# Attention, MoE and MoE2 fused on one core: MoE2's second products by seven in all four groups of sets 0 and 1, recombined at the set's end

## The chip, the cores and the metric

The kernel runs on one core of one Trainium2 chip. The metric is device time in microseconds (us) of one execution, as the median of repeated runs. The core has five engines with a queue each, and each queue runs strictly in its own order: TensorE (PE, matrix products), VectorE (DVE), ScalarE (ACT), GpSimd (POOL) and SyncE (SP, which here issues nearly all transfers). They wait for each other by semaphores.

## What is computed

The reference, cut to what matters:

```python
# attention in chunks of 64 rows: B, H, S, D = 4, 8, 576, 64
scores = q_c @ k_c.T / sqrt(D);  attn = softmax(scores);  x = attn @ v_c   # -> x: 2304 x 512
# MoE, 4 experts, hidden size 1024
p = domain_probs / (domain_probs.sum(-1) + 1e-9)
out = sum_e p[:, e] * (relu(x @ w1[e]) @ w2[e])                            # 2304 x 512
# MoE2, hidden size 2048
h = out @ w_in;  g = h * clip(h + 3, 0, 6) / 6
result = g @ w_out                                                         # 2304 x 512
```

## The kernel before

**Precision.** PE multiplies in a rounded form of float32 (fp32r). Each operand is split into a high part (a cast on ACT) and a low part (the difference, on DVE or POOL), and each product is three matmuls: high by high, high by low, low by high. So every operand costs one ACT instruction and one DVE or POOL instruction before PE may use it.

**Sets, groups, units.** The 2304 tokens are three sets of 768, and each set is two halves of N = 384 tokens (index z). The hidden columns are groups of 512: eight for MoE (phase 0), four for MoE2 (phase 1). A unit is one group of one set: first the h products (x by the first weights), then a gate, then the y products (gate by the second weights). Phase 0 runs set 0, 1, 2, then phase 1 runs set 0, 1, 2. The attention of set 0 fills the start of the program, and that of sets 1 and 2 is done in small pieces beside MoE.

**Products by seven.** All h products but those of the first unit use a scheme of Strassen's kind: seven half-size products instead of eight, of sums of blocks. In `h_pair` (L971 and after) they are asked for in the order P1, P6, P7, P5, P2, P4, P3, twice for each unit (two pairs), six matmuls of 384 columns each (L989), and DVE recombines them (L999). Their x operands are built once for each set by `build_x`: seven high parts on ACT (L703, 768 columns, or L707), fourteen low halves on DVE (L711, 384 columns), and eight differences of 384 columns on DVE (L717), 22 DVE steps in all. P6 needs the difference called t2 (both halves, in place in the tile xs), and P5 and P4 need differences too. The seven operands have one buffer each (the slots of x7), so that an operand of the next set can be written only after the last product of the present set has read that slot.

**The y products.** In MoE2 the units g = 0, 1, 2 of every set do their y products by seven as well (`y_sevens`, L1167: 126 matmuls of 256 columns), with sums of gate blocks made by `gate_sums` (L1112) and split by `parts` (L1103, L1105). The seven results M1 to M7 are added up over the groups in tiles called totals (acc, tri, vr, qr, kr; copies at L1180, additions at L1182), and `recombine` (L1196, seven additions of 256 columns for each of three row blocks j) turns them into plain accumulators at the end of group 2. Group 3 is plain (`y_unit`, L1221: 72 matmuls of 512 columns): its results are added to the accumulators by `finish` (L1265) and sent out (L1282).

**The order.** Nothing is ordered by hand. `Plan` takes every operation with an engine, a length by a formula, a due time and its dependencies, plays them through, and emits the instructions in the order of the starts it found. On an engine the ready operation with the earliest due time goes first. Operations marked `pair` (both inputs in SBUF) are put 8 us later on DVE while POOL is busy (`YIELD`), and are taken to last longer by a share of what POOL still has to do (`SHARED`). The tables at the top of the file (L20 and after) shift due times and lengths. `build_x` for phase 1 is due 12 us ahead of its unit.

Of the kernel before, what the change touches and what calls it, by code (L numbers as in the profile page):

```python
# [18 lines left out]

W_LEAST = 2.0 ** -15  # L20
W_MOST = 122880.0 - 2.0 ** -6
Y0 = 18.74
SLACK = (6.73, 4.93, 5.97, 0.92)
LOADS = (((0.0, 0.0), (0.4, 0.55)), ((4.0, 4.0), (4.1, 4.1)), ((9.0, 9.0), (9.1, 9.1)))

ITEMS = (56.47, 23.57, -37.2, 3.52)
STAGES = (12.74, -112.55)
LEAD = (14.98, 23.38, 6.6, 8.16)
LOAD = 13.67
BACK = (("pyy", "ppp"), ("pyp", "ppp"))  # L30
CO = ("POOL","POOL","DVE")
FIRST = 271.53
KEPT = 1.15
EARLY = 12.94
RGAP = 7.28
PLAIN_STAY = (1, 3)
STAY = (("A12", 0), ("A12", 1), ("A22", 0))
S4_STAY = (0,)
SUMS = 1.53
YB = ("yyy","ahy","yhh","ahh")  # L40
LATER = 3.06
LO = 0.81
VLOADS = (1.0, 6.0, 12.0)
SH = (0.0, 0.0, 0.0)
BANKS = (("hhhhh", "yahay"), ("ayaay", "yyyay"), ("ayaay", "ayaay"))
# [2 lines left out]
def raw(ap):  # L48
    return ap.bitcast(F32)
# [23 lines left out]
class Plan:  # L73
# [3 lines left out]
    LAT = 0.3  # L77
    EVERY = 0.6
    DENSE = 7.7
    CALM = 5.19  # L80
    LANES = 8
    SHARED = 0.87
    YIELD = 8

# [16 lines left out]
    def run(self):  # L101
        free = dict(self.caps)
        ready = {e: [] for e in ("PE", "DVE", "ACT", "POOL", "SP")}
        busy = dict.fromkeys(ready, 0.0)
# [16 lines left out]
        done, position, now = 0, 0, 0.0  # L121
# [32 lines left out]
        def choose(e):  # L154
            if e == "PE":
                nxt = self.main[position] if position < len(self.main) else None
                able = nxt is not None and nxt.left == 0 and any(r is nxt for r in ready[e]) and room(nxt)
                sides = sorted((r for r in ready[e] if r.side), key=lambda r: (r.due, r.n))
                for s in sides:
                    if (s.due <= now or not able) and fits(s):  # L160
                        return s
                return nxt if able else None
            able = sorted(ready[e], key=lambda r: (r.due, r.n))
            if e == "DVE" and busy["POOL"] > now + 0.15 and able:

# [24 lines left out]
        while done < len(self.ops):  # L190
# [19 lines left out]
            for e in ready:  # L210
                if busy[e] > now + 1e-9 or not (ready[e] or e == "PE" and now < self.warm):
                    continue
                o = choose(e)
                if o is None:
                    if e == "PE" and filled < now < self.warm:
                        fill(now)
                        filled = now + (self.EVERY if now >= self.DENSE else 0.0)
                    continue
                ready[e].remove(o)
                for b in o.new:  # L220
                    free[b.tag] -= 1
                    heads[b.tag] += 1
                o.start = now
                busy[e] = now + o.us
                if o.pair and e == "DVE":

                    busy[e] += self.SHARED * max(busy["POOL"] - now, 0.0)
                if e == "PE" and not o.side:
                    position += 1
                end = busy[e]  # L230
                if o.lag:
                    pipe = max(pipe, end) + o.lag
                    end = pipe + 1.9 + o.slack
                    sent.append(pipe + 1.9)
                    seq += 1
                    heapq.heappush(events, (sent[-1], seq, 2, o))
                o.end = end
                seq += 1
                heapq.heappush(events, (end, seq, 1, o))
                seq += 1  # L240
                heapq.heappush(events, (busy[e], seq, 2, o))
# [16 lines left out]
def fused_kernel(ctx: ExitStack, tc: tile.TileContext, q, k, v, probs, w1, w2, win, wout, out):  # L258
# [5 lines left out]
    P = 128  # L264
# [93 lines left out]
    HP = 42  # L358

    YS = 14  # L360
    by_seven = lambda u: u[0] == 1 and u[2] < G2 - 1
    hus_of = lambda u: 48 * mm(2 * u[4]) if u[4] < N else 2 * HP * mm(N)
    START = 22.0
    clock, at = START, {}
# [458 lines left out]
    def split_y(ph, g, R, ld, due):  # L823
# [23 lines left out]
        T3 = sub(s3, r(1, 1), r(0, 1), ld, [R], 4.1)  # L847
        operand("M7", whole(s3), [s3], [T3], 5)
        operand("M3", r(1, 1), [R], ld, 6)
        return los  # L850

    def weights(ph, si, g):
# [5 lines left out]
        if (ph, si) != (0, 0):  # L858
# [2 lines left out]
                wready[key, name] = op("SP", 0.35, lambda b=b, name=name: nc.sync.dma_start(out=raw(b.t), in_=raw(kept[ph, g, name])), t - LEAD[0] + j, [stored[ph, g, name]], [b], lag=1.35, hold=hold)  # L861
            for n_, f in enumerate(YO if by_seven((*key, 0, N)) else FO):
                tag = YO.get(f, "wy")
                if tag != "e":
                    b = wo[key, "y", f] = buf(tag)
                    wready[key, "y", f] = op("SP", 0.35, lambda b=b, f=f: nc.sync.dma_start(out=raw(b.t), in_=raw(kept[ph, g, f])), t_y - LEAD[3] + n_, [stored[ph, g, f]], [b], lag=1.35, hold=hold_y)
# [280 lines left out]
    def y_sevens(u):  # L1147
# [6 lines left out]
        for q_, pair in enumerate(Y_PAIRS):  # L1154
# [19 lines left out]
            for j in range(NJ):  # L1174
# [6 lines left out]
                else:  # L1181
                    x = op("DVE", dve(w) + 0.08, lambda T=T, p=ps[j], w=w: nc.vector.tensor_tensor(out=T.t[:, :w], in0=p.t[:, :w], in1=T.t[:, :w], op=ALU.add), t + n_ * one + LATER - soon(u), [last[j], before], (), [T, ps[j]])  # L1182
                totals[k_] = (T, x)
        if g == G2 - 2:
            for j in range(NJ):
                recombine(si, j, t + n_ * one - soon(u) + RGAP * j, CO[j])

    def recombine(si, j, due, eng):

# [17 lines left out]
    def y_unit(u, z, ending=False):  # L1207
# [8 lines left out]
        for f, j in todo:  # L1216
            W, (G, lo, o) = wo[key, "y", f], gts[u, f, z]

            def fn(f=f, j=j, W=W, G=G, o=o):
                for i, (a, b) in enumerate(HL):  # L1220
# [1 line left out]
                        ps[j].t, G.t[:, a, o + j * P:o + (j + 1) * P], W.t[:, b, :],  # L1222
                        start=f == FO[0] and i == 0, stop=f == FO[-1] and i == len(HL) - 1,
                    )
            last[j] = op("PE", 3 * mm(512), fn, t, [wready[key, "y", f], lo], [ps[j]] if f == FO[0] else (), [W, G, ps[j]])
        end = t + len(js) * GF * 3 * mm(512)
        for j in js:
            finish(u, z, j + c0 // P, ps[j], last[j], end - (len(js) - 1 - j) * 3 * mm(512) * (GF if ending else 1), ending and j == len(js) - 1)
# [159 lines left out]
    for n_, u in enumerate(units):  # L1388
        ph, si, g, c0, n = u
        if ph == 1 and g == 0:  # L1390
# [3 lines left out]
            for b in range(P // R32):  # L1394
# [2 lines left out]
                    in_=x2s[si][:, b::P // R32].rearrange("r k z t -> r k (z t)"),  # L1397
                )
                lds.append(op("SP", 0.5, load, t - 30, x2ready[si], () if b else [X], [X], lag=1.0, hold=t - 60))
            build_x((1, si), lds, t - 12)  # L1400
        if is_plain(u):
            for f in range(GF):
                for zs in ((0, 1),) if n < N and n_ else ((0,), (1,)) if n_ else ():
# [51 lines left out]
```

## Time and profile before

| | before |
|---|---|
| median of 3 runs | 1178.86 us (1178.58 to 1183.39) |
| the profiled execution | 1178.26 us, span 1176.4 us |
| PE busy | 1160.3 us, 99% |
| DVE / ACT / POOL busy | 744.9 / 491.1 / 517.8 us |
| granted TensorE clock | 1.0 over the whole span (2.4 GHz) |
| DMA | 317.04 MB, mean 269 GB/s |

PE is the engine to look at: whatever adds or removes PE work, or makes PE wait, moves the end, and busy time on the others does so only through a wait of PE. The span minus PE's busy time is 16.1 us; most of that lies in the first 60 us and in the last 4. In MoE2, from 812.8 us on, PE has no gap at all before the tail.

### The profile page before, as it was taken

To read this page: it belongs to the slowest core of one execution; us is meant where nothing else is said; L and a number is where in the kernel's file an instruction comes from. 1 tells how busy PE (TensorE), PEld (TensorE's weight loads), DVE (VectorE), ACT (ScalarE), POOL (GpSimd) and SP (SyncE) were. 2 spreads that over 40 slices of the span, in tenths; PEclk is the share of its full clock that TensorE was granted. 3 is DMA by queue.
4 is the path that set the end of the run, shared out by engine and by line. 5 is a ranking of instruction groups with operands and counts; after the bars stand their busy time and mean duration, and the time that the engine had idled before them with its cause. 6 is when DMAs were issued, how large, how long until landed. Compare 5 with 4: busy or idle time off the path is not lost.

```text
span 1176.4 us, 20820 instructions
## 1 busy us (share of the span) xinstructions
PE 1160.3 (99%) x7488; PEld 1067.0 (91%) x7488; DVE 744.9 (63%) x1465; ACT 491.1 (42%) x1178; POOL 517.8 (44%) x458
## 2 busy tenths in 40 slices
PE   7999999999999999999999999999999999999998
PEld 7899988889998888888999999888999899989997
DVE  5565455458655666679645555468478846884685
ACT  5754444445344332435232333233534453345332
POOL 3576656555242253536243434341447044704470
PEclk9999999999999999999999999999999999999999
DMA  9678888768887998887978787987797678768751
GB/s 248 221 275 289 306 262 297 271 232 314 292 293 244 294 344 306 281 293 258 332 270 309 253 304 243 307 331 248 275 296 251 229 269 291 264 224 278 251 179 55
DMA packets 155783, 317.04 MB, mean 269 GB/s; under 512 B 70688, under 2 KB 77088, under 8 KB 155680
## 3 DMA queue, kind: packets, MB, share of 16 engines
q1 hardware_dynamic: 153936, 314.01, 78.8%
q10 hardware_dynamic: 1744, 1.70, 0.5%
q8 instruction: 59, 0.97, 0.3%
q14 instruction: 44, 0.36, 0.1%
HBM read 232.30 MB, written 83.36 MB: 268 GB/s over the span
## 4 chain that ended last, share of the span: by engine, by line
PE 92%; DVE 3%; DMA 2%; issue 1%; SPq 0%; ACT 0%; POOL 0%; DVEq 0%; POOLq 0%; ACTq 0%
PE h L989 40%; PE y L1221 36%; PE y L1167 5%; PE h L1167 4%; PE a L1167 2%; DMA k<-wp 2%; PE h L1048 2%; DVE x L711 1%; DMA wy<-k 1%; PE y L318 1%; PE a L567 1%; PE y L487 0%; PE h L576 0%; DVE gt L1073 0%; DVE xs L717 0%
## 5 line engine op out<-in xcount | busy, mean ns | idle before, releaser
L989 PE MATMUL h<-x,wh 128*128 128x384 f32 x2940 | 522.6, 335 | 2.4 <-DVE c L999 1.0
L989 PEld LDWEIGHTS h<-x,wh 128*128 128x128 f32 x2940 | 509.6, 188 | 7.7 <-DVE c L999 2.3
L1221 PE MATMUL y<-wy,gt 128*128 128x512 f32 x1944 | 454.2, 391 | 2.7 <-DVE acc L1258 2.6
L1221 PEld LDWEIGHTS y<-wy,gt 128*128 128x128 f32 x1944 | 362.2, 188 | 78.9 <-DVE acc L1258 4.0
L1258 DVE SCALAR_TENSOR_TENSOR acc<-y,pn,acc 128x512 f32<-128x512 f32 x126 | 89.0, 749 | 125.5 <-PE y L1221 125.3
L1105 POOL TENSOR_TENSOR gt<-t,gt 128x384 fp32r<-128x384 f32 x54 | 54.5, 1017 | 187.4 <-ACT gt L1103 187.1
L999 DVE TENSOR_TENSOR h<-h,c 128x384 f32<-128x384 f32 x152 | 84.5, 562 | 43.4 <-PE h L989 42.3
L1072 ACT ACTIVATE gt<-h 128x384 fp32r<-128x384 f32 (+1 forms) x150 | 68.8, 486 | 100.2 <-DVE h L999 99.5
L925 POOL TENSOR_TENSOR w<-w,rh 128x512 f32<-128x512 f32 x28 | 37.1, 1326 | 154.3 <-DVE rh L922 110.2
L999 DVE TENSOR_TENSOR c<-h,p 128x384 f32<-128x384 f32 x70 | 38.8, 554 | 91.9 <-PE h L989 62.3
L1073 DVE SCALAR_TENSOR_TENSOR gt<-h,gt 128x384 fp32r<-128x384 f32 (+1 forms) x150 | 76.6, 540 | 31.3 <-ACT gt L1072 29.6
L1006 ACT COPY p<-h 128x384 f32<-128x384 f32 x70 | 33.6, 480 | 124.3 <-PE h L989 123.9
L782 POOL TENSOR_TENSOR wp<-t,wp 128x512 fp32r<-128x512 f32 x36 | 47.1, 1308 | 72.4 <-ACT wp L780 72.4
L1080 ACT ACTIVATE t<-h,half 128x384 f32<-128x384 f32 x84 | 45.9, 579 | 53.8 <-DVE h L999 42.1
L782 POOL TENSOR_TENSOR wy<-t,wy 128x512 fp32r<-128x512 f32 x32 | 41.7, 1310 | 38.6 <-ACT wy L780 37.3
L782 POOL TENSOR_TENSOR wp<-rh,wp 128x512 fp32r<-128x512 f32 x24 | 32.1, 1336 | 55.8 <-ACT wp L780 55.8
L1167 PE MATMUL y<-wy,gt 128*128 128x256 f32 x432 | 56.1, 283 | 0.0
L1167 PEld LDWEIGHTS y<-wy,gt 128*128 128x128 f32 x432 | 54.1, 191 | 0.0
L780 ACT CAST wp<-t 128x512 fp32r<-128x512 f32 x36 | 22.4, 623 | 67.7 <-DMA k<-wp 47.3
L999 DVE TENSOR_TENSOR c<-h,c 128x384 f32<-128x384 f32 x70 | 38.8, 554 | 18.0 <-PE h L989 17.4
L711 DVE TENSOR_TENSOR x<-xs,x 128x384 fp32r<-128x384 f32 x66 | 42.8, 669 | 1.6 <-ACT x L703 1.6
L1103 ACT CAST gt<-t 128x384 fp32r<-128x384 f32 x66 | 32.7, 513 | 24.8 <-POOL t L1112 19.0
(209 smaller groups left out, 1435.7 us busy)
## 6 DMA issues: line engine op xcount, KB each, us to landing
wh<-k SPq DMA_DIRECT2D x196, 512.0 KB, 5.9
wy<-k SPq DMA_DIRECT2D x112, 512.0 KB, 5.2
k<-wp SPq DMA_DIRECT2D x60, 512.0 KB, 6.3
k<-wh SPq DMA_DIRECT2D x49, 512.0 KB, 3.6
k<-wy SPq DMA_DIRECT2D x32, 512.0 KB, 4.7
wp<-k SPq DMA_DIRECT2D x18, 512.0 KB, 4.4
t<-in_moe_w_dram SPq DMA_DIRECT2D x32, 256.0 KB, 4.4
rh<-in_moe_w_dram SPq DMA_DIRECT2D x8, 1024.0 KB, 7.7
```

The costliest lines, as they stand in the source:

```text
L711: lo = lambda k=k: nc.vector.tensor_tensor(out=b.t[:, 1, k], in0=src[k](), in1=raw(b.t[:, 0, k]), op=ALU.subtract)
L782: return op(eng, gps(512) if eng == "POOL" else dve(512), lambda: e.tensor_tensor(out=view(b.t[:, 1]), in0=read(), in1=raw(view(b.t[:, 0]) ...
L925: nc.gpsimd.tensor_tensor(out=low(), in0=low(), in1=dst(), op=ALU.mult)
L989: nc.tensor.matmul(acc.t[:, :n], W.t[:, a, k_ * 256 + pr_ * P:k_ * 256 + (pr_ + 1) * P], X.t[:, b, k_, cs], start=new and first, stop=last ...
L999: add = lambda out, x, y: (lambda: nc.vector.tensor_tensor(out=out(), in0=x(), in1=y(), op=ALU.add))
L1072: hi = op("ACT", act(n), lambda: nc.scalar.activation(hi_(), src(), AF.Relu), due, after, [G], bufs)
L1073: lo = op("DVE", dve(n), lambda: nc.vector.scalar_tensor_tensor(out=lo_(), in0=src(), scalar=0.0, in1=raw(hi_()), op0=ALU.max, op1=ALU.sub ...
L1080: x = op("ACT", act(n), lambda: nc.scalar.activation(r_(), src(), AF.Relu, bias=half, scale=1.0 / 6.0), due, after, [R], bufs)
L1105: lo = op(eng, dve(N) if eng == "DVE" else gps(N), lambda: e.tensor_tensor(out=where()[:, 1], in0=r_(), in1=raw(where()[:, 0]), op=ALU.sub ...
L1167: nc.tensor.matmul(ps[j].t[:, 256 * i:256 * i + 256], Gs[k][2]()[:, a, j * P:(j + 1) * P], part(b)[:, 256 * k:256 * k + 256], start=k == 0 ...
L1221: nc.tensor.matmul(ps[j].t, G.t[:, a, o + j * P:o + (j + 1) * P], W.t[:, b, :], start=f == FO[0] and i == 0, stop=f == FO[-1] and i == len ...
L1258: fn = lambda: nc.vector.scalar_tensor_tensor(out=A.t, in0=ps.t, scalar=p, in1=A.t, op0=ALU.mult, op1=ALU.add)
```

## The change

What it does, part by part:

- `by_seven` now holds for all groups of MoE2 but the last group of the last set. So group 3 of sets 0 and 1 does its y products by seven, and its weights are split into seven blocks (`split_y`) instead of four plain ones. For the plain group of set 2, `split_y` also stores M0, and `weights` puts each plain block together from two halves (two loads of 256 columns).
- `recombine` moves to the end of group 3 in sets 0 and 1, and the outputs are sent right after it from `y_sevens`. In set 2 it stays at the end of group 2. All three row blocks are recombined on POOL (`CO`); before, the third was on DVE.
- In `Plan`, `YIELD` and `SHARED` take effect only after 60 us of the plan (`BEGUN`), so that the first attention items are ordered by due times alone.
- `build_x` for phase 1 is due 22.88 us (`XD`) ahead instead of 12, and about twenty numbers of the tables differ.

The diff, cut to its core (lines of after.py are 3 to 19 higher than those of before.py: L711, L717, L999, L1182, L1196 become L714, L720, L1012, L1195, L1214):

```diff
-CO = ("POOL","POOL","DVE")
+CO = ("POOL","POOL","POOL")
+XD = 22.88
+RD = 4.75
...
+    BEGUN = 60
...
-            if e == "DVE" and busy["POOL"] > now + 0.15 and able:
+            if e == "DVE" and now > self.BEGUN and busy["POOL"] > now + 0.15 and able:
...
-                if o.pair and e == "DVE":
+                if o.pair and e == "DVE" and now > self.BEGUN:
...
-    by_seven = lambda u: u[0] == 1 and u[2] < G2 - 1
+    by_seven = lambda u: u[0] == 1 and u[1:3] != (NSET - 1, G2 - 1)
...
+        if not by_seven((ph, NSET - 1, g, 0, N)):
+            operand("M0", r(0, 1), [R], ld, 7)
...
+                if ph and f not in YO:
+                    b = wo[key, "y", f] = buf(tag)
+                    blocks = wready[key, "y", f] = []
+                    for d, name in enumerate((("M1", "M0"), ("M2", "M3"))[f % 2]):
+                        fn = lambda b=b, d=d, name=name, k=f // 2: nc.sync.dma_start(out=raw(b.t)[:, :, 256 * d:256 * d + 256], in_=raw(kept[ph, g, name])[:, :, 256 * k:256 * k + 256])
+                        blocks.append(op("SP", 0.35, fn, t_y - LEAD[3] + n_, [stored[ph, g, name], *blocks], () if d else [b], [b], lag=0.7, hold=hold_y))
+                    continue
...
-        if g == G2 - 2:
+        if g == G2 - 1 - (si == NSET - 1):
             for j in range(NJ):
-                recombine(si, j, t + n_ * one - soon(u) + RGAP * j, CO[j])
+                due = t + n_ * one - soon(u) + RGAP * j + RD
+                recombine(si, j, due, CO[j])
+                for z in range(2 if g == G2 - 1 else 0):
+                    A = accs[1, si, z, j]
+                    for ps_, rows in out_runs(si, z, j):
+                        op("SP", 0.5, lambda A=A, ps_=ps_, rows=rows: nc.sync.dma_start(out=rows, in_=A.t[ps_]), due + 24, [aready[1, si, z, j]], (), [A], lag=1.3 * (ps_.stop - ps_.start) / P)
...
-            build_x((1, si), lds, t - 12)
+            build_x((1, si), lds, t - XD)
```

**Where instructions move: DVE at the end of MoE2's set 0.** Before, these are the last steps for set 1's x operands (L717 differences, L711 low halves), the additions of group 3's results (L1265), and the first two sums of the next unit's h products (L999):

```order
L1265 TENSOR_TENSOR acc<-y,acc 128x512 x3
L717 TENSOR_TENSOR xs<-xs 128x384
L711 TENSOR_TENSOR x_65<-xs,x_65 128x384
L717 TENSOR_TENSOR xs<-xs 128x384
L711 TENSOR_TENSOR x_65<-xs,x_65 128x384 x2
L717 TENSOR_TENSOR xs<-xs 128x384
L711 TENSOR_TENSOR x_65<-xs,x_65 128x384 x5
L1265 TENSOR_TENSOR acc<-y,acc 128x512 x3
L999 TENSOR_TENSOR c<-h,p_10452 128x384
L999 TENSOR_TENSOR c<-h,c 128x384
```

Now, on the same engine and at the same place; the first row adds M3's last result of the unit (its PE product is the unit's last):

```order
L1195 TENSOR_TENSOR kr<-h,kr 128x256
L720 TENSOR_TENSOR xs<-xs 128x384
L714 TENSOR_TENSOR x_65<-xs,x_65 128x384
L720 TENSOR_TENSOR xs<-xs 128x384
L714 TENSOR_TENSOR x_65<-xs,x_65 128x384 x3
L720 TENSOR_TENSOR xs<-xs 128x384
L714 TENSOR_TENSOR x_65<-xs,x_65 128x384 x2
L720 TENSOR_TENSOR xs<-xs 128x384
L714 TENSOR_TENSOR x_65<-xs,x_65 128x384
L1012 TENSOR_TENSOR c<-h,p_10530 128x384
L1012 TENSOR_TENSOR c<-h,c 128x384
L714 TENSOR_TENSOR x_65<-xs,x_65 128x384 x2
```

Thirteen of the 22 x steps now stand behind the unit's last addition, and eleven of them ahead of the next unit's first sum. The end of set 1 has the same rows. On POOL, the 21 additions of `recombine` stand in one row there, between the last split of the unit and the first of the next.

**The same place on ACT.** Before, the casts for the x operands (L703), then the copy of the next unit's first product P1 (L1006):

```order
L1103 CAST gt<-h 128x384 x2
L1080 ACTIVATE t<-h,half 128x384 x2
L1103 CAST gt<-h 128x384 x2
L703 CAST x_65<-xs 128x768 x4
L1006 COPY p_10452<-h 128x384
L1080 ACTIVATE t<-h,half 128x384 x2
```

Now (L706 is the cast, L1019 the copy):

```order
L1116 CAST rh<-t 128x384
L1116 CAST w_10439<-h 128x384
L706 CAST x_65<-xs 128x768
L1019 COPY p_10530<-h 128x384
L706 CAST x_65<-xs 128x768 x3
L1093 ACTIVATE t<-h,half 128x384 x2
```

Three casts, those of P6, P5 and P4, now stand behind the copy of P1's result.

**DVE in the first attention items.** Before; L755 makes the low part of an x operand for the first unit, L529 to L559 belong to attention items:

```order
L557 TENSOR_REDUCE st<-e 128x8
L558 TENSOR_TENSOR st<-st,least 128x8
L559 RECIPROCAL st<-st 128x8
L529 TENSOR_REDUCE st<-y 128x4 x2
L755 TENSOR_TENSOR x_65<-xs,x_65 128x2x2x128
L533 TENSOR_TENSOR st<-st,minus 128x8
```

Now:

```order
L560 TENSOR_REDUCE st<-e 128x8
L561 TENSOR_TENSOR st<-st,least 128x8
L562 RECIPROCAL st<-st 128x8
L758 TENSOR_TENSOR x_65<-xs,x_65 128x2x2x128
L532 TENSOR_REDUCE st<-y 128x4 x2
L536 TENSOR_TENSOR st<-st,minus 128x8
```

The low part moved ahead of the two maxima. On POOL at the same place the weighing of an item (L563) moved ahead of the first split of a second weight (L782).

## Rows read from the trace of the kernel before

**Rows 1.** The page, part 1: busy us (share of the span) and instructions.

```profile
PE 1160.3 (99%) x7488; PEld 1067.0 (91%) x7488; DVE 744.9 (63%) x1465; ACT 491.1 (42%) x1178; POOL 517.8 (44%) x458
```

**Rows 2.** Waits of PE: who waited for whom, us in total, times, longest.

```profile
PE y L1221 <- DVE acc L1258: 2.6, 2, 1.4
PE h L1048 <- DVE x L755: 1.6, 1, 1.6
```

**Rows 3.** Windows: us, busy of each engine, clock, DMA share and GB/s.

```profile
20.00:40.00 20.00, 18.16 (x290) 15.59 (x288) 10.96 (x27) 14.49 (x46) 9.78 (x10) 1.00 1.00 287
528.00:561.00 33.00, 31.48 (x156) 27.64 (x155) 31.04 (x51) 16.47 (x32) 18.72 (x13) 1.00 0.78 269
700.00:804.00 104.00, 102.22 (x506) 90.80 (x504) 62.77 (x118) 31.85 (x61) 38.85 (x30) 1.00 0.88 307
812.80:932.80 120.00, 120.00 (x787) 116.97 (x787) 88.26 (x172) 54.31 (x109) 50.02 (x53) 1.00 0.77 258
```

**Rows 4.** Windows of a unit by seven and of set 0's plain unit.

```profile
842.47:872.12 29.65, 29.65 (x211) 29.65 (x211) 20.19 (x38) 11.91 (x25) 12.97 (x13) 1.00 0.73 261
901.76:932.79 31.03, 31.03 (x158) 28.00 (x157) 29.37 (x59) 13.85 (x25) 6.79 (x9) 1.00 0.55 182
```

**Rows 5.** Windows of the y products alone: by seven, then plain.

```profile
857.03:872.12 15.09, 15.09 (x127) 15.09 (x127) 12.75 (x25) 5.30 (x12) 6.99 (x7) 1.00 0.91 334
916.32:932.79 16.47, 16.47 (x74) 13.44 (x73) 15.60 (x32) 6.73 (x11) 0.00 (x0) 1.00 0.58 191
```

**Rows 6.** Chain of waits in order of time: start, us; P1 of MoE2's group 2.

```profile
872.12 1.04 PE h L989 x6
```

**Rows 7.** Timeline of DVE: start us, us, instruction [idle before, releaser].

```profile
872.15 0.42 DVE L1182 TENSOR_TENSOR kr<-h,kr 128x256 f32<-128x256 f32 x1 [0.29 <-PE h L1167]
928.17 2.43 DVE L711 TENSOR_TENSOR x<-xs,x 128x384 fp32r<-128x384 f32 x5
903.02 0.85 DVE L1196 TENSOR_TENSOR acc<-acc 128x256 f32<-128x256 f32 x1
903.90 0.84 DVE L1196 TENSOR_TENSOR acc<-acc,tri 128x256 f32<-128x256 f32 x1
905.14 0.49 DVE L1196 TENSOR_TENSOR acc<-tri 128x256 f32<-128x256 f32 x1
546.63 1.18 DVE L711 TENSOR_TENSOR x<-xs,x 128x384 fp32r<-128x384 f32 x1
```

**Rows 8.** Timeline of POOL.

```profile
544.53 1.30 POOL L837 TENSOR_TENSOR t<-rh,t 128x512 f32<-128x512 f32 x1
547.36 1.61 POOL L837 TENSOR_TENSOR t<-t,rh 128x512 f32<-128x512 f32 x1
898.97 1.46 POOL L1196 TENSOR_TENSOR tri<-tri,acc 128x256 f32<-128x256 f32 x2 [2.37 <-DVE tri L1182]
903.55 0.92 POOL L1196 TENSOR_TENSOR acc<-acc,tri 128x256 f32<-128x256 f32 x1
907.89 0.74 POOL L1196 TENSOR_TENSOR acc<-acc,qr 128x256 f32<-128x256 f32 x1
```

**Rows 9.** Timeline of SP: issue of transfers, first start, time over all.

```profile
924.27 6.26 SPq L1282 DMA_DIRECT2D out_dram<-acc  x12
941.17 5.52 SPq L861 DMA_DIRECT2D wh<-k  x6
```

**Rows 10.** Timeline of the start, DVE, POOL and PE.

```profile
23.68 1.15 DVE L558 TENSOR_TENSOR st<-st,least 128x8 f32<-128x8 f32 x1
26.90 1.68 DVE L755 TENSOR_TENSOR x<-xs,x 128x512 fp32r<-128x512 f32 x1
23.52 1.29 POOL L782 TENSOR_TENSOR wy<-t,wy 128x512 fp32r<-128x512 f32 x1 [6.84 <-ACT wy L780]
25.21 1.04 POOL L563 TENSOR_TENSOR e<-e,st 128x512 f32<-128x512 f32 x1 [0.40 <-DVE st L559]
28.64 0.86 PE L1048 MATMUL h<-x,wh 128*128 128x256 f32 x5 [1.55 <-DVE x L755]
```

More of the change, by code (lines that the diff above doesn't have):

```diff
@@ L21 @@
 W_MOST = 122880.0 - 2.0 ** -6
-Y0 = 18.74
-SLACK = (6.73, 4.93, 5.97, 0.92)
+Y0 = 18.86
+SLACK = (6.67, 5.48, 6.22, 0.94)
 LOADS = (((0.0, 0.0), (0.4, 0.55)), ((4.0, 4.0), (4.1, 4.1)), ((9.0, 9.0), (9.1, 9.1)))
[L26 to L29, printed above, removed]
+ITEMS = (52.06, 27.71, -38.72, 3.66)
+STAGES = (21.63, -99.84)
+LEAD = (15.54, 25.07, 6.41, 7.16)
+LOAD = 15.89
 BACK = (("pyy", "ppp"), ("pyp", "ppp"))
-CO = ("POOL","POOL","DVE")
[L32 to L36, printed above, removed]
+CO = ("POOL","POOL","POOL")
+FIRST = 275.4
+KEPT = 0.51
+EARLY = 8.94
+XD = 22.88
+RD = 4.75
+RGAP = 2.05
+PLAIN_STAY = (2, 3)
 STAY = (("A12", 0), ("A12", 1), ("A22", 0))
 S4_STAY = (0,)
-SUMS = 1.53
+SUMS = 2.62
 YB = ("yyy","ahy","yhh","ahh")
-LATER = 3.06
-LO = 0.81
+LATER = -2.6
+LO = 0.83
 VLOADS = (1.0, 6.0, 12.0)
@@ L79 @@
     DENSE = 7.7
-    CALM = 5.19
+    CALM = 5.49
     LANES = 8
+    BEGUN = 60
     SHARED = 0.87
@@ L1224, in fn @@
                     )
-            last[j] = op("PE", 3 * mm(512), fn, t, [wready[key, "y", f], lo], [ps[j]] if f == FO[0] else (), [W, G, ps[j]])
+            wrdy = wready[key, "y", f]
+            last[j] = op("PE", 3 * mm(512), fn, t, [*(wrdy if isinstance(wrdy, list) else [wrdy]), lo], [ps[j]] if f == FO[0] else (), [W, G, ps[j]])
         end = t + len(js) * GF * 3 * mm(512)
```

## The prediction

> **What bounds the kernel now.** The page's busy times come first: PE is busy for 1160.3 of 1176.4 us and no other engine for more than two thirds [rows 1]. So an edit counts only if it changes PE's work or makes PE wait. The waits of PE come second: the long ones are single events of 1.4 to 1.6 us [rows 2]. The windows come third, and show where they lie: 1.84 us of PE's idle time in 20 to 40 us, 1.52 around the change from set 1 to set 2 of MoE, 1.78 before MoE2, and none in a whole set of MoE2 [rows 3]. There the units follow each other without a gap, 29.65 us by seven and 31.03 plain [rows 4]. The question is therefore what the two new units by seven take off PE, and whether MoE2 stays without gaps.
>
> **PE's work.** The y products take 15.09 us by seven and 16.47 plain [rows 5]. Two units change: 2 x 1.38 = 2.76 us less. That is work, not a wait, and certain.
>
> **The end of sets 0 and 1.** Here the order decides. Before, the 22 x steps for the next set stood inside the plain unit, all of them ahead of its last three additions, on a DVE that was busy for 29.37 of 31.03 us, while POOL had only its recombination (6.79 us, over early in the unit) [rows 4]. Now the unit is by seven. A unit by seven without x steps keeps DVE busy for 20.19 us [rows 4]. Five x steps in a row take 2.43 us, 0.47 each after the first [rows 7], so 22 add 10.4. That is 30.6 us of work for a unit of 29.65, without any collision with POOL, which now has 13 us of sums and splits in the same unit [rows 4]. DVE cannot finish, and the order shows what was put off: behind the last addition (kr) stand t2's two halves, the low halves of P6, and more, eleven x steps ahead of the next unit's first sum. On ACT the cast of P6 stands behind the copy of P1's result. P6 is the second product that PE wants.
>
> I count from T, the start of the next unit's P1, which is also the end of the old unit's last product [rows 6]. The addition kr cannot be over before T + 0.45: 872.15 + 0.42, less 872.12 [rows 6, 7]. The second low half of P6 is the eighth x step after it. PE wants it with P6's fifth matmul, at 1.04 + 4/6 x 1.04 = T + 1.73 [rows 6].
>
> How long is an x step? Undisturbed 0.47, which gives T + 0.45 + 8 x 0.47 = 4.21 and a wait of 2.5 us. But POOL is in the middle of 21 recombination steps. Where DVE and POOL both did such steps of 256 columns, DVE started one every 0.88 us (903.02, 903.90) [rows 7] and POOL's took 0.92 instead of 0.74 [rows 8]. An x step has 128 columns more, at most 0.16 us (a third of 0.47): 0.88 to 1.04, and I take 1.0. The x step of 1.18 us among POOL's steps of 512 columns [rows 7, 8] is near it. P6 is then complete at 0.45 + 8.0 = T + 8.45, a wait of 6.7 us. After it P5 wants the eleventh step (T + 11.45) for its fifth matmul, which would come at 8.45 + 0.35 + 1.04 + 0.69 = 10.53: 0.9 more. P4 wants the thirteenth, behind two sums of 0.47: 0.45 + 13.0 + 0.94 = 14.4, against 11.45 + 0.35 + 1.04 + 0.69 = 13.5: 0.9 more. In all 8.5 us. POOL is at it for so long: 18 of its 21 steps come after the first tri addition, which was at 898.97 in a unit that began at 872.12 [rows 6, 8], 26.85 us in; at 0.8 each four are done by T, and fourteen of 1.0 last until about T + 14.
>
> Inside the unit, too, nine x steps stand among the sums of the h products and of the gates. At the two set changes of MoE, where all 22 stand beside POOL's work, PE lost 1.52 and up to 1.78 us [rows 3]; nine of 22 give 0.7. Bounds: 0 and 1.8.
>
> So each of the two set ends costs 8.5 + 0.7 = 9.2 us, with 2.5 and 10.3 as bounds from these rows: two cost 18.4 (5 to 20.6).
>
> The Trainium skill ("SBUF — State Buffer", section "Who interferes with whom") says that a VectorE instruction with two SBUF inputs and a GpSimd instruction that reads SBUF exclude each other for the whole instruction. The trace agrees that they hinder each other, but not for the whole of it: 0.88 per pair where the sum of both would be more. With full exclusion a step would be 0.74 + 0.47 = 1.21; that is a rival below.
>
> **The other parts.** The outputs of a set are now 24 transfers in a row on SP, 0.52 us each (6.26 for 12) [rows 9], behind the recombination and ahead of the seven loads of wh, which before began 8.4 us into the unit (941.17 less 932.79) [rows 4, 9]. The last outputs can go at about T + 14 and take 2 to 4 us, so wh for the next unit comes some 10 us later than before, 20 us ahead of its use at T + 38: 0, and it would only cost if the recombination were another 10 us later. The next unit's totals need the acc buffers that these outputs hold, at T + 19 before and at T + 27 with PE late: 0. The first splits of the next unit wait on POOL behind the recombination until T + 14; their inputs are late by 8.5 us themselves, so 0.
>
> The new weights of group 3 cost eight more POOL steps of 1.3 us [rows 8] and four casts, in MoE, where POOL is idle more than half of the time [rows 1]: 0, at worst one wait like the 1.4 in [rows 2]. Their loads lie where DMA was busy for 0.55 of the time [rows 4]: 0. The halved loads of set 2's last weights move the same bytes: 0. The third row block of set 2's recombination on POOL instead of DVE ends some 6 us later, 10 us ahead of the first addition to it: 0.
>
> At the start, L558 took 1.15 us because POOL's first split stood in its way, and the low part L755 came behind two maxima and took 1.68 [rows 10]. Now POOL weighs first, and L755 goes ahead. POOL's weighing can then start about 1 us earlier (24.2), be over at 25.3, and the split at 26.6; the low part collides with the split and ends about 27.2, where it ended at 28.58. PE's wait of 1.55 [rows 10] shrinks to about 0.2. Some of it returns at the first gate: ACT's casts for it come behind the exponentials, which still wait for those maxima. I take 1.2 us less, with 1.84 less (all idle time of that window [rows 3]) and 1.0 more (a collision like that of L558) as bounds.
>
> The rest of MoE is planned anew by other numbers. Its order has the same shape at the set changes, so I take 0, with 3.3 to either side (the 1.52 and 1.78 of [rows 3] gone, or twice).
>
> **Sum.** 1178.26 (the profiled execution: its span of 1176.4 and 1.9 around it) - 2.76 - 1.2 + 18.4 = 1192.7. The median of the runs lies 0.6 above the profiled one, so 1193.3 us.
>
> **The rivals.**
> - *Undisturbed steps.* POOL yields and DVE's x steps keep their 0.47. Each set end costs 2.5, nothing follows: + 5.0 - 2.76 - 1.2 gives 1179.3, or 1179.9 as a median: no change. For it: one of DVE's recombination steps took 0.49 beside POOL. Against it: others took 0.84 and 0.85 [rows 7]. That P6 waits at all is not in doubt, as the order puts kr ahead of t2.
> - *Full exclusion.* Steps of 1.21, and 1.8 inside the unit. P6 at 0.45 + 9.7, a wait of 8.4, P5 and P4 1.4 each: 13.0 for each set end, 26.0 - 3.96: 1200.9. It decides if the one always waits for the whole of the other's step.
> - *Half.* DVE slips in ahead of POOL in part, steps of 0.75: P6 waits 4.7, the followers 0.5, the unit 0.7: 5.9 each, 11.8 - 3.96: 1186.7.
> - *Faster.* Other side: PE's saving stays, the start gives its 1.84, and MoE loses its two stalls: - 2.76 - 1.84 - 3.3 would be 1171.0 if the set ends cost nothing. For that, t2 would have to be ready before kr; DVE's queue forbids it, and with the least wait of 5.0 it is 1176. Only an operand that P6 did not need would decide for this.
>
> **Chances.** The forecast 0.55, full exclusion 0.15, half 0.17, undisturbed 0.10, faster 0.03. About 0.5% (5.9 us) is what a measurement of this kernel can tell from no change. Slower by more than that (over 1184.8): 0.55 + 0.15 + 0.17 = 0.87. Within it: the undisturbed case and most of the faster one, 0.11. Faster: 0.02. The forecast's own bounds are 1188 and 1199; half of the full exclusion and most of the half case belong to the 8 in 10, so the range is 1183 to 1200.
>
> **What would show it.** Right: at both set ends of MoE2's first two sets PE is idle for 6 to 8 us between the first product of a set (P1) and the second (P6), released by DVE's L714, with POOL's L1214 busy beside it; about 1 us more before P5 and P4; x steps of 0.9 to 1.1 us there; y blocks of 15.1 us in all eleven units by seven; the wait for L758 at 27 us shorter than 0.5 us. Wrong: no PE gap at T + 1, x steps of 0.5 us beside POOL, or gaps of this size elsewhere, in the plain unit of set 2 or in MoE.

## The result and the profile after

The changed kernel takes 1197.53 us (median; 1195.82 to 1199.39), the one before 1179.47 beside it: a ratio of 1.015, 95% interval 1.0133 to 1.0167. The forecast was 1193.3 us, slower by more than 0.5%. The profiled execution took 1196.27 us, its span 1194.5, 18.1 more than before.

The page's busy times and the waits of PE (us in total, times, longest) come first, as before [rows 1, 2]:

```profile
PE 1166.9 (98%) x7596; PEld 1076.8 (90%) x7596; DVE 765.2 (64%) x1458; ACT 497.5 (42%) x1194; POOL 579.5 (49%) x513
```

```profile
PE h L1002 <- ACT x L706: 5.6, 2, 2.8
PE h L1002 <- DVE x L714: 4.8, 4, 1.7
PE h L1002 <- DVE gt L1086: 1.9, 1, 1.9
PE a L1180 <- ACT gt L1116: 1.2, 2, 0.6
PE a L1180 <- DVE gt L1118: 1.0, 2, 0.5
PE h L1061 <- DVE x L758: 0.5, 1, 0.5
```

The first two rows are new and belong to the ends of MoE2's sets 0 and 1: one wait for ACT and two for DVE's L714 at each. The fourth and fifth, new too, lie in the unit before each end, and the third is one wait in MoE, at 370 us. PE's busy time went up by 6.6 us although it has 2.76 us less work; part of it ran at a lower clock. The windows (us, PE's busy time, granted clock, DMA share, GB/s) show both set ends, from group 3's h products to the y products of the next set, and two y blocks by seven elsewhere:

```profile
901.32:956.04 54.72, 48.44 (x296) 0.94 0.59 193
985.68:1000.77 15.09, 15.09 (x128) 1.00 0.97 325
1030.42:1085.38 54.96, 48.60 (x296) 0.94 0.56 185
1144.68:1159.76 15.08, 15.08 (x127) 1.00 0.74 247
```

Without a gap such a stretch takes 29.65 + 14.56 = 44.21 us [rows 4, 5]. So the set ends cost 10.51 and 10.75, 21.26 together. MoE2 began at 812.22 in place of 812.77, and everything behind the second set end is without gaps as before. That is the whole account: 1178.26 - 2.76 (y products) + 21.26 - 0.55 = 1196.2.

PE's timeline at the first set end (start, us, matmuls, idle time before and its releaser), then DVE's and POOL's, show how:

```profile
921.24 0.50 PE L1180 MATMUL a<-wy,gt 128*128 128x256 f32 x2 [0.59 <-ACT gt L1116]
922.25 0.39 PE L1180 MATMUL a<-wy,gt 128*128 128x256 f32 x1 [0.51 <-DVE gt L1118]
...
932.79 1.21 PE L1002 MATMUL h<-x,wh 128*128 128x384 f32 x6
936.80 0.45 PE L1002 MATMUL h<-x,wh 128*128 128x384 f32 x1 [2.79 <-ACT x L706]
938.93 1.33 PE L1002 MATMUL h<-x,wh 128*128 128x384 f32 x3 [1.69 <-DVE x L714]
940.94 15.10 PE L1002 MATMUL h<-x,wh 128*128 128x384 f32 x74 [0.68 <-DVE x L714]
```

```profile
918.07 1.20 DVE L714 TENSOR_TENSOR x<-xs,x 128x384 fp32r<-128x384 f32 x1
...
933.01 0.41 DVE L1195 TENSOR_TENSOR kr<-h,kr 128x256 f32<-128x256 f32 x1
933.34 0.54 DVE L720 TENSOR_TENSOR xs<-xs 128x384 f32<-128x384 f32 x1
933.80 1.08 DVE L714 TENSOR_TENSOR x<-xs,x 128x384 fp32r<-128x384 f32 x1
934.80 1.07 DVE L720 TENSOR_TENSOR xs<-xs 128x384 f32<-128x384 f32 x1
935.80 3.08 DVE L714 TENSOR_TENSOR x<-xs,x 128x384 fp32r<-128x384 f32 x3
938.80 1.08 DVE L720 TENSOR_TENSOR xs<-xs 128x384 f32<-128x384 f32 x1
939.80 2.08 DVE L714 TENSOR_TENSOR x<-xs,x 128x384 fp32r<-128x384 f32 x2
```

```profile
936.42 1.04 POOL L1214 TENSOR_TENSOR acc<-acc,tri 128x256 f32<-128x256 f32 x1
937.43 1.03 POOL L1214 TENSOR_TENSOR acc<-tri 128x256 f32<-128x256 f32 x1
938.43 1.04 POOL L1214 TENSOR_TENSOR acc<-acc,tri 128x256 f32<-128x256 f32 x1
```

Behind kr DVE starts an x step every 1.00 us (the first after 0.46), and POOL a step of its recombination every 1.00: the two take turns, step by step. PE's first gap ends with ACT's cast for P6, which itself waits for the third of these steps, t2's second half. P6's two low halves are the sixth and the eighth; at the end of each PE goes on. The granted clock behind the gaps (windows, PE alone, columns as above):

```profile
936.80:938.90 2.10, 0.44 (x1) 0.89 0.17 42
938.90:940.94 2.04, 1.33 (x4) 0.50 0.46 118
940.94:943.00 2.06, 2.06 (x6) 0.50 0.44 110
943.00:945.00 2.00, 2.00 (x8) 0.50 0.32 79
945.00:947.00 2.00, 2.00 (x12) 0.93 0.54 138
```

From about 938.4 to 945.3 us (0.22 of the first of these windows, three whole ones, 0.14 of the last) PE had the lower of its two levels, 1.2 GHz, and a matmul took twice as long. Before that it had stood for 2.79 us, done one matmul, and stood again.

### The profile page after: what moved, and what is told of

Read it like the earlier page. It is cut to its first block, busy times and chain, and to the rows that moved or that the text cites. A ratio compares the mean times of both kernels' runs of the same rounds, so it can differ in the third digit from the quotient of the medians.

```text
span 1194.5 us, 21159 instructions
## 1 busy us (share of the span) xinstructions
PE 1166.9 (98%) x7596; PEld 1076.8 (90%) x7596; DVE 765.2 (64%) x1458; ACT 497.5 (42%) x1194; POOL 579.5 (49%) x513
## 4 chain that ended last, share of the span: by engine, by line
PE 87%; DVE 9%; ACT 2%; DMA 2%; issue 1%; SPq 0%; POOL 0%; DVEq 0%; ACTq 0%; POOLq 0%
PE h L1002 40%; PE y L1239 32%; PE y L1180 5%; PE h L1180 4%; DVE x L714 2%; DVE xs L720 2%; PE a L1180 2%; DMA k<-wp 2%; PE y L321 0%; DVE acc L1195 0%; PE h L1061 0%; PE a L570 0%; DVE h L1012 0%; PE h L579 0%; DVE x L758 0%
## 5 line engine op out<-in xcount | busy, mean ns | idle before, releaser
L1002 PE MATMUL h<-x,wh 128*128 128x384 f32 x2940 | 529.5, 338 | 12.8 <-ACT x L706 5.6
L1002 PEld LDWEIGHTS h<-x,wh 128*128 128x128 f32 x2940 | 515.8, 190 | 18.7 <-DVE x L714 6.4
L1239 PE MATMUL y<-wy,gt 128*128 128x512 f32 x1800 | 422.0, 392 | 3.2 <-DVE acc L1277 2.5
L1239 PEld LDWEIGHTS y<-wy,gt 128*128 128x128 f32 x1800 | 335.1, 188 | 74.5 <-DVE acc L1277 3.8
L1118 POOL TENSOR_TENSOR gt<-t,gt 128x384 fp32r<-128x384 f32 x66 | 67.3, 1028 | 134.1 <-ACT gt L1116 134.1
L938 POOL TENSOR_TENSOR w<-w,rh 128x512 f32<-128x512 f32 x32 | 42.4, 1324 | 172.1 <-DVE rh L935 140.9
L1012 DVE TENSOR_TENSOR h<-h,c 128x384 f32<-128x384 f32 x152 | 84.6, 561 | 39.8 <-PE h L1002 38.8
L1012 DVE TENSOR_TENSOR c<-h,p 128x384 f32<-128x384 f32 x70 | 38.9, 555 | 81.5 <-PE h L1002 75.0
L1019 ACT COPY p<-h 128x384 f32<-128x384 f32 x70 | 33.7, 481 | 109.0 <-PE h L1002 109.0
L1180 PE MATMUL y<-wy,gt 128*128 128x256 f32 x528 | 68.6, 283 | 0.0
L785 POOL TENSOR_TENSOR wp<-rh,wp 128x512 fp32r<-128x512 f32 x28 | 36.9, 1318 | 64.5 <-ACT wp L783 64.5
L1180 PEld LDWEIGHTS y<-wy,gt 128*128 128x128 f32 x528 | 66.2, 191 | 0.0
L714 DVE TENSOR_TENSOR x<-xs,x 128x384 fp32r<-128x384 f32 x66 | 54.3, 842 | 6.1 <-ACT x L706 6.1
L1012 DVE TENSOR_TENSOR c<-h,c 128x384 f32<-128x384 f32 x70 | 38.7, 553 | 19.0 <-PE h L1002 18.0
L1125 POOL TENSOR_TENSOR t<-t 128x384 f32<-128x384 f32 x44 | 45.8, 1041 | 5.7 <-DVE t L1094 4.0
```

The costliest lines, as they stand in the source:

```text
L714: lo = lambda k=k: nc.vector.tensor_tensor(out=b.t[:, 1, k], in0=src[k](), in1=raw(b.t[:, 0, k]), op=ALU.subtract)
L785: return op(eng, gps(512) if eng == "POOL" else dve(512), lambda: e.tensor_tensor(out=view(b.t[:, 1]), in0=read(), in1=raw(view(b.t[:, 0]) ...
L1002: nc.tensor.matmul(acc.t[:, :n], W.t[:, a, k_ * 256 + pr_ * P:k_ * 256 + (pr_ + 1) * P], X.t[:, b, k_, cs], start=new and first, stop=last ...
L1012: add = lambda out, x, y: (lambda: nc.vector.tensor_tensor(out=out(), in0=x(), in1=y(), op=ALU.add))
L1118: lo = op(eng, dve(N) if eng == "DVE" else gps(N), lambda: e.tensor_tensor(out=where()[:, 1], in0=r_(), in1=raw(where()[:, 0]), op=ALU.sub ...
L1125: return op(eng, dve(N) if eng == "DVE" else gps(N), lambda: e.tensor_tensor(out=dst.t[:, :N], in0=x.t[:, :N], in1=y.t[:, :N], op=op_), du ...
```

## The experiments

The price of a set end below is the stretch from group 3's h products to the next set's y products in the trace, less 44.21. The changed kernel has 10.51 and 10.75. Times are medians, ratios are to the kernel before, measured beside it.

| kernel | us | ratio (95%) | set ends, us |
|---|---|---|---|
| e1 group 3 plain | 1177.76 | 0.9987 (0.9976 to 0.9997) | none by seven |
| e2 no recombination | 1186.89 | 1.0069 (1.0047 to 1.0091) | 4.84, 4.84 |
| e3 x steps of 768 | 1191.85 | 1.0101 (1.0076 to 1.0126) | 8.33, 8.02 |
| e4 wait filled | 1197.57 | 1.0155 (1.0137 to 1.0174) | 10.42, 10.42 |
| e5 both of these | 1187.40 | 1.0061 (1.0044 to 1.0079) | 6.26, 6.27 |
| e6 half steps on POOL | 1195.62 | 1.0126 (1.0100 to 1.0153) | 9.34, 8.61 |
| e7 old start rule | 1198.05 | 1.0149 (1.0119 to 1.0179) | 10.59, 10.83 |
| e8 old numbers | 1209.96 | 1.0251 (1.0220 to 1.0282) | 10.84, 10.83 |
| e9 two moves in MoE | 1177.30 | 0.9980 (0.9965 to 0.9994) | none by seven |
| e10 casts behind gates | 1178.27 | 0.9979 (0.9969 to 0.9989) | none by seven |

**e1, the main part undone.**

```
-    by_seven = lambda u: u[0] == 1 and u[1:3] != (NSET - 1, G2 - 1)
+    by_seven = lambda u: u[0] == 1 and u[2] < G2 - 1
...
-                if ph and f not in YO:
+                if ph and f not in YO and by_seven((ph, 0, g, 0, N)):
...
-        if g == G2 - 1 - (si == NSET - 1):
+        if g == G2 - 2:
```

> Group 3 of sets 0 and 1 is plain again, with its x steps and its recombination where a plain unit has them; the new numbers, the new start and the replanned MoE stay. Theory A (the two set ends make the loss, by what the unit by seven puts beside the x steps): from the start of MoE2 to the last unit the changed kernel lost 9.21 us at the first set end and 9.35 at the second, so 1197.5 - 18.6 = 1178.9 us, PE without a gap at both set ends, and 0.55 us won before MoE2 is all that is left of the change. Theory B (the new numbers, such as the earlier due time of the x steps, make the loss in any unit): 1190 or more, with gaps of several us behind P1.

1177.76, and both stretches have at most 0.09 us of idle time in all. They take 46.08 us each, 0.49 more than the 31.03 + 14.56 = 45.59 before [rows 4, 5]; what makes this half microsecond is not shown:

```profile
899.30:945.38 46.08, 46.00 (x243) 1.00 0.63 208
1019.76:1065.84 46.08, 45.99 (x243) 1.00 0.64 209
```

The set ends by seven make the loss, not the new numbers in themselves. What is left of the change, 0.13%, is a small gain.

**e2, POOL's share.** In `recombine` a step of sets 0 and 1 does nothing: `lambda: si == NSET - 1 and e.tensor_tensor(...)`.

> The 21 recombination steps of POOL at the end of set 0 and of set 1 are left out (those of set 2 stay); all other instructions stand in the same order on every engine. Theory A (each x step waits for one POOL step, 1.00 us in place of 0.47): P6's second low half is ready at T + 0.45 + 8 x 0.47 = T + 4.2 in place of T + 8.15, PE's gaps behind P1 sum to 2.5 us in place of 5.16, and behind them nothing is late; the 1.8 us lost inside the unit stay, since POOL's splits stand there. 4.3 in place of 10.6 for each set end: 1197.5 - 12.6 = 1185 us. Theory B (the order of DVE's work makes the loss, and its steps are slow for another reason): the x steps stay at 1.0 us and the time at 1197.

1186.89. DVE's three x steps in a row, which took 3.08 us in the changed kernel, and PE behind its gap:

```profile
936.76 1.54 DVE L714 TENSOR_TENSOR x<-xs,x 128x384 fp32r<-128x384 f32 x3
```

```profile
937.77 14.62 PE L1002 MATMUL h<-x,wh 128*128 128x384 f32 x78 [1.74 <-ACT x L706]
```

The x steps are back at 0.47 us, the clock stays at 1.00 and 2.85 us are lost behind the start of P1 in place of 8.53. The order is the same, so POOL's steps are 5.7 and 5.9 us of the two set ends. What the order alone costs stays: 2.85, and 1.99 inside the unit. No run put t2's steps ahead of kr by hand, so what a better order would win is not shown.

**e3, longer DVE instructions.** In `build_x` the first of two x steps does nothing in MoE2 and the second does both halves. For the low halves, with the differences likewise: `k and nc.vector.tensor_tensor(out=b.t[:, 1], in0=src[2](), in1=raw(b.t[:, 0]), op=ALU.subtract)`.

> In MoE2 two x steps of 384 columns become one of 768 at the place of the second, the rest of the order is kept; the elements are the same. Theory A (DVE and POOL take turns, one instruction each, and a POOL step of 256 columns holds DVE up for 1.00 - 0.47 = 0.53 us whatever DVE's length): a step of 768 takes 0.90 + 0.53 = 1.43, four of them behind kr 5.7, P6 complete at T + 6.2 in place of T + 8.15; about 2.3 us less behind T and 0.4 less in the unit at each end: 1192 us. Theory B (both engines run at about half speed while they run together, by the element): 768 columns take 2.0 us and the time stays at 1197. Theory C (the one waits for the whole of the other's instruction as it lasts undisturbed, 0.74): 1.64 for a step, P6 at T + 7.0, 1195 us.

```profile
934.68 4.28 DVE L714 TENSOR_TENSOR x<-xs,x 128x768 fp32r<-128x768 f32 x3
...
942.93 0.56 DVE L1012 TENSOR_TENSOR c<-h,c 128x384 f32<-128x384 f32 x1 [0.70 <-PE h L1002]
```

```profile
939.00 16.48 PE L1002 MATMUL h<-x,wh 128*128 128x384 f32 x77 [2.86 <-DVE x L714]
```

1191.85, with steps of 1.41 us (938.87 to 940.28; 0.87 undisturbed, 925.41 to 926.28): theory A, and neither half speed (2.0) nor the whole of POOL's step (1.64). The x step of 768 columns is held up by 0.54 us, that of 384 by 0.53: one turn of POOL each. But 77 matmuls took 16.48 us where 13.36 would do, at a granted clock of 0.50 until about 945 us, and now DVE waits for PE.

**e4, the clock held.** Thirty matmuls on P1's operands into P6's bank, overwritten by P6, fill the wait (the lines behind stand one lower, L1003 is L1002; `more_` is set only for P6 of the first pair at the two set ends):

```
+   not k_ and more_ and [nc.tensor.matmul(acc.t[:, :n], more_[0].t[:, 0, pr_ * P:(pr_ + 1) * P], xo[(ph, si), "P1"].t[:, 0, 0, cs], start=True, stop=True) for _ in range(30)]
```

> Thirty matmuls of 384 columns, whose result is thrown away, stand between P1 and P6 at the two set ends (30 x 0.1735 = 5.2 us inside a wait that ends 6.9 us after P1), so that TensorE works through most of it. The changed kernel ran the stretch behind the wait at a granted clock of 0.50 for some 6.6 us. Theory A (DVE's supply sets the pace there: at full clock PE would wait 0.8 us for P5's and 0.7 for P4's last low half, which is ready at T + 13.86): the clock stays at 1.00, these two waits appear, and each end gains only 0.7: 1196 us. Theory B (the lower clock costs time of its own): 3.4 us less at each end, 1190.7. If the clock falls all the same: 1197.5.

```profile
936.08 5.36 PE L1000 MATMUL h<-x,wh 128*128 128x384 f32 x30
941.28 0.86 PE L1003 MATMUL h<-x,wh 128*128 128x384 f32 x4
943.25 2.36 PE L1003 MATMUL h<-x,wh 128*128 128x384 f32 x12 [1.11 <-DVE x L714]
946.28 2.62 PE L1003 MATMUL h<-x,wh 128*128 128x384 f32 x12 [0.67 <-DVE x L714]
949.11 9.07 PE L1003 MATMUL h<-x,wh 128*128 128x384 f32 x50 [0.21 <-DVE x L714]
```

1197.57: the clock stayed at 1.00, and the waits for P6's, P5's and P4's last low halves stand there. The two that the prediction had counted at 0.9 each are 0.67 and 0.21. So in the changed kernel the lower clock cost almost nothing: it filled time in which PE would have waited for DVE.

**e5, both.** The edits of e3 and e4, with 26 matmuls.

> The x steps of 768 columns and, between P1 and P6 at the two set ends, 26 matmuls whose result is thrown away (4.5 us). With the steps of 768 alone P6 was ready at T + 5.8 in place of T + 8.15, but the y products began only 0.95 us earlier at the first set end: the granted clock stood at 0.50 for some 5 us behind the wait, and DVE waited for PE there (0.70, 0.30 and 1.41 us). Theory A (in that kernel the lower clock, not DVE, sets the pace behind P6): at full clock P5 waits about 0.6 and P4 0.3, and the y products begin 2.2 us earlier at each end: 1191.9 - 4.4 = 1187.5 us. Theory B (DVE's supply sets it, as in the changed kernel, where filling the wait won nothing): 1191.9.

1187.40. One gap of 0.44 us is left behind the filling, and the set ends fell by 2.07 and 1.75 against e3. With a faster DVE the lower clock does cost time; filling the wait, worth nothing in e4, is worth 3.8 us here. Even so the kernel stays 0.6% slower than before the change.

```profile
937.16 11.55 PE L1003 MATMUL h<-x,wh 128*128 128x384 f32 x65 [0.44 <-DVE x L714]
```

**e6, shorter POOL instructions.** Each step of `recombine` in sets 0 and 1 is done as `slice(0, 128)` and `slice(128, 256)`.

> Each recombination step of POOL in sets 0 and 1 becomes two of 128 columns, the order and the elements are the same. Theory A (a POOL step holds an x step up for a time that goes with its columns): 0.27 us of 0.53, an x step takes 0.74 to 0.80, P6 is ready at T + 6.6 in place of T + 8.15; of that a bit under half arrives at the y products, as with the steps of 768: about 1 us for each end, 1195.5. Theory B (each POOL instruction holds one x step up for a fixed 0.53, however small it is): steps of 1.0 us as before, and twice as many of POOL's, which then hinder for longer: 1197.5 to 1200.

```profile
937.91 2.26 DVE L714 TENSOR_TENSOR x<-xs,x 128x384 fp32r<-128x384 f32 x3
```

An x step takes 0.73 us: 0.26 of waiting for 128 columns, 0.53 for 256. That is theory A. The set ends in the trace are 1.17 and 2.14 us shorter; the time of 1195.62 alone does not show it, as its interval and that of the changed kernel overlap.

**e7, the start rule.** `BEGUN = 0` in place of 60.

> The plan yields to POOL from the first microsecond, as before the change; the tables are those of the changed kernel, so the attention's first items stand as they stood before, and MoE is planned anew from there. Theory A (the rule alone gives the 1.05 us by which PE idles less in the first 60 us): PE's wait for the low part L758 is 1.5 us again in place of 0.47, the first 60 us lose about 1 us, and the rest changes by its replanned stalls, some +-2 us: 1198.5. Theory B (the start was won by the tables): no change in the first 60 us, 1197.5.

```profile
PE h L1061 <- DVE x L758: 1.6, 1, 1.6
```

The wait of 0.47 is 1.6 again, so the rule shortens it, not the tables. The time of 1198.05 doesn't tell 1 us apart: in its profiled run (1201.12 us) the first 40 us had a clock of 0.91, and a wait of 5.67 us ended at 376.67, where the profiled run of the changed kernel has one of 1.95. What the rule is worth in all stays open.

**e8, the change with the old numbers.** All tables as before the change.

> Group 3 by seven in sets 0 and 1, recombined at the set's end, and the new start rule, but all tables as before the change: the x steps are due 12 us ahead of the set in place of 22.88, the recombination at the end of the products and its third row block on DVE. Theory A (no numbers help, since DVE has 30.6 us of work in a unit of 29.65 and POOL's steps beside it): a similar number of x steps stands behind kr, each set end costs 9 to 13 us: 1195 to 1202. Theory B (the new numbers put the x steps wrongly and make the loss): 1180.

1209.96, outside of both theories. The set ends cost the same (10.84, 10.83), as theory A has it. But MoE2 began at 820.96, 8.74 us later than in the changed kernel, and its first y block waited once for a load of weights:

```profile
852.33 1.62 PE L1180 MATMUL y<-wp,rh 128*128 128x256 f32 x6 [4.49 <-DMA wp<-k]
```

So the new numbers don't help at the set ends; they win 12 us elsewhere. That this is the price of group 3's additional weight work by the old numbers is argued: e8 has the new start rule too, and was not run without the weight work. Its trace fits. Its longest wait in MoE, 2.93 us at 375.86, is for an ACT copy that stands behind a cast of a weight block, and that cast had waited 6.83 for a store. Which of the numbers does it was not tried.

**e9 and e10, a better version.** In the changed kernel and in e1 an ACT cast of a weight block waited 6 us for the store of its buffer, ahead of two gates in ACT's queue (ACT's timeline, changed kernel):

```profile
368.75 0.62 ACT L783 CAST wp<-t 128x512 fp32r<-128x512 f32 x1 [6.02 <-DMA k<-wp]
369.28 0.86 ACT L1085 ACTIVATE gt<-h 128x384 fp32r<-128x384 f32 x2
```

Both runs start from e1; the starts of single instructions, in the plan's own time, are set behind `plan.run()`:

```
e9:  cast L783 364.80 -> 366.75, its split to 366.76; x step 546.76 -> 550.10
e10: cast L783 364.80 -> 369.70, the next 371.55 -> 373.70, their splits with them; x step as in e9
```

> Group 3 plain in all sets, with the new start and numbers, and two instructions put later by hand in MoE: the ACT cast of a weight block (L783) at 365 us goes behind the two gates L1085, for in that kernel it waited 6.1 to 6.6 us for the store of its buffer and held the gates back (PE's wait of 1.83 at 369.9); and one x step of DVE (L714, 551.03, 1.64 us long beside POOL's 512 columns) goes behind the three additions to acc, of which PE wanted the first at 552.06 (its wait of 1.33 at 553.4). Theory A (each wait goes with what stood in front): 1.8 and 0.9 us less, 1177.8 - 2.7 = 1175 us, 0.4% below the kernel before. Theory B (what was put behind is late next: POOL's split and the next stores, or P7's low half): the two waits turn up elsewhere, 1177 to 1179.

> As the run before, but the cast that was moved goes behind all four gates L1085 and the next cast behind the two that follow (at 370 and 374 us), so that no cast that waits for the store of its buffer stands ahead of a gate there; the x step behind the three additions stays moved. In the run before the wait at 369.9 and that at 553.4 had gone, but the same cast then stood at 371.64 ahead of the gates for y, and 1.51 + 1.02 us of new waits on L1086 came at 381 to 383 us. Theory A (a waiting cast ahead of a gate is the whole cause): those go too, PE idles under 0.5 us between 365 and 385, 1175 us. Theory B (the stores are late for the blocks behind them as well, on SP and POOL): new waits of 1 to 3 us on the weights or the attention items behind, 1177 to 1179.

In e9 the waits at 369.9 and 553.4 went, and the cast held up the next gates (ACT's timeline of e9); in e10 those are free and an attention item is late, whose exponentials stand behind a later cast on ACT (ACT's, then PE's timeline of e10):

```profile
371.64 0.62 ACT L783 CAST wp<-t 128x512 fp32r<-128x512 f32 x1 [3.68 <-DMA k<-wp]
```

```profile
383.83 0.62 ACT L783 CAST wp<-rh 128x512 fp32r<-128x512 f32 x1 [6.22 <-DMA k<-wp]
```

```profile
388.39 0.90 PE L570 MATMUL a<-ident,e 128*128 128x128 f32 x3 [3.50 <-POOL e L566]
```

Theory B holds both times: the stores of that stretch are late, and the wait goes to whatever stands behind a cast. The three versions with a plain group 3 (e1, e9, e10) can't be told apart. Each is 0.1 to 0.2% faster than the kernel before, and some 1.6% faster than the changed one.

## Why the prediction was right

Its forecast and its mechanism held: DVE's x steps for P6 stand behind kr, take 1.00 us each beside POOL, and PE waits for them. The sum of 1192.7 was 3.6 us too small against the profiled run, 2.6 of it in one term. The set ends, 10.51 and 10.75, lie above the bound of 10.3 that it gave them, and its bounds of 1188 and 1199 have no working: those of its terms add up to about 1176 and 1201. By its steps:

- *PE's work*: 15.09 and 15.08 us per y block where nothing waits, as said.
- *kr and the x steps.* The timeline starts a row while the one before drains (it has group 3's h products at 901.15, the chain at 901.32), so T is 932.79 + 0.17 = 932.96. kr was over at 933.42, T + 0.46 (0.45 said). The steps took 1.00 us (1.0 said), but the first only 0.46. P6 was complete at 940.84, T + 7.9 (8.45 said). PE lost 6.2 us there (6.7 said): 2.79 + 1.69 + 0.68 in gaps, and 1.09 because the four matmuls between them show 1.78 in their rows, not 0.69, three of them at the lower clock. It had looked for one wait of 6 to 8 us, released by DVE's L714; the longest of the three gaps is released by ACT's cast.
- *P5 and P4*, 0.9 each: in the changed kernel there is no such gap; 74 matmuls took 15.10 in place of 12.84, 2.26 more. The place of these waits was taken by the lower clock, which the prediction did not have. e4 shows that they are there without it, at 0.67 and 0.21 behind a longer wait for P6. Behind T the set end lost 8.53 (8.5 said). That these agree is luck: P6 cost 0.5 less than said, and the lower clock 0.5 more than the two waits in whose place it came.
- *Inside the unit*, 0.7 with bounds of 0 and 1.8: this is the term that was mis-sized. It is 1.99 (901.15 to 932.79 is 31.64, less 29.65), at both set ends. 1.10 of it are the two gaps at 921 and 922, for gates that DVE and ACT had late behind x steps of up to 1.20 us beside POOL's splits. All of it lies in the y block, where DVE was busy for 16.93 of 17.07 us. The set changes of MoE, from which the term was scaled, are plain units, and DVE's share there is as high (31.04 of 33.00 us [rows 3]); why a unit by seven loses more is not shown beyond these late gates. Wide steps cut it to 0.75 (e3: 902.79 to 933.19); leaving out the recombination didn't change it. Two set ends, 1.3 more each: 2.6 of the 3.6 us.
- *Start*, -1.2: PE was busy for 53.81 of the first 60 us in place of 52.76, -1.05. POOL weighed at 24.04 (24.2 said), L758 ended at 26.87 (27.2), and PE waited 0.47 for it (0.2).
- *Rest of MoE*, 0 +- 3.3: it took 0.5 of the start's gain back in this run. The set change from 1 to 2 has 1.74 us of idle time in 528 to 561 us (1.52 before [rows 3]), the stretch before MoE2 1.14 (1.78). A new one came at 370 us: 1.95 here, and 0.66 to 3.89 in e2 to e6, which have the same order there. Behind it the granted clock fell as well, and 42 matmuls took 9.12 us instead of 7.45 (PE's timeline), so this stall cost some 3.6 us. In e5, behind a wait of 0.66, the clock stayed at 1.00 and they took 7.55; that run (1184.47) is the fastest of its seven. Stalls of this kind spread the times by a few us.

```profile
361.01 7.45 PE L1002 MATMUL h<-x,wh 128*128 128x384 f32 x42
370.41 9.12 PE L1002 MATMUL h<-x,wh 128*128 128x384 f32 x42 [1.95 <-DVE gt L1086]
```

- *Costed at nothing*: the 24 outputs stood on SP from 937.49 to 952.41 and wh was loaded behind them, 18.6 us ahead of its use (20 said). The weights of group 3 cost little: e1, without them, began MoE2 at 810.30, 1.92 us earlier; 1.14 of that is the stall before MoE2. That they cost little holds with the new tables; with the old ones the same change is 12 us slower (e8).

Of the rivals, undisturbed steps are out (1.00, not 0.47), and so is *half* (0.75). Full exclusion at 1.21 is out as a price, but not as a rule. The Trainium skill ("SBUF — State Buffer", section "Who interferes with whom") has the two engines exclude each other. The trace agrees: they alternate, and DVE's length adds in full (0.87 + 0.54 = 1.41 in e3). What it does not bear out is the length of POOL's turn, 0.53 for a step whose row is 0.74 long when nothing disturbs it [rows 8]. How much of that row is reading is not shown. *Faster* failed as the prediction said: DVE's queue has kr ahead of P6's steps.

## What to carry to other kernels

Before work is moved into a unit, add up what each engine has to do between two deadlines of the bounding engine, with the collisions in it: here DVE had 30.6 us for 29.65 even undisturbed, and 1.38 us saved on PE cost 10.6. Where DVE and POOL must work side by side, make DVE's instructions long and POOL's short, since each DVE instruction with both inputs in SBUF waited for one of POOL's; a sum that reads a product (L1012 at 943.83) kept its 0.55. In these runs a lower clock behind a wait cost only where the engine that feeds PE was ahead; measure it with the wait filled before counting it.

## What the runs showed of the hardware

- An x step on DVE is held up by POOL for 0.26 us by steps of 128 columns, 0.53 by 256, and about 1.1 by 512 (an x step every 1.56 us, 549.47 to 551.03 in e1's timeline, less 0.47), whatever DVE's own length (0.53 and 0.54 for 384 and 768 columns beside POOL's 256): it goes with POOL's columns, at some 2.1 ns each, without a fixed part that would show. DVE and then POOL in e1's timeline, POOL at 512 columns:

```profile
549.47 1.64 DVE L714 TENSOR_TENSOR x<-e,x 128x384 fp32r<-128x384 f32 x1
551.03 1.64 DVE L714 TENSOR_TENSOR x<-vr,x 128x384 fp32r<-128x384 f32 x1
```

```profile
549.09 1.60 POOL L785 TENSOR_TENSOR wp<-t,wp 128x512 fp32r<-128x512 f32 x1
550.66 1.59 POOL L840 TENSOR_TENSOR t<-t,rh 128x512 f32<-128x512 f32 x1
```

- After gaps of 2.79 and 1.69 us with one matmul between them TensorE was granted 0.50 for some 6.8 us; after a gap of 1.74 us (e2) it kept 1.00, as it did with the gap filled (e4). At 370 us one gap of 1.95 us (changed kernel) was followed by some 3.4 us at 0.50: windows of 2 us from 370 to 376 have 0.96, 0.50 and 0.69. What separates it from the gap in e2 is not shown.
- Waiting for the same store in the same order, ACT's cast at 368 to 372 us was late by amounts that made PE wait 0.66 to 3.89 us from run to run. What on the DMA side makes the difference stays open.
